# Gated mix of linear attention and expert lookup: where masks, numerators and output matmuls stand from tile 2 on

## The chip, the cores and the metric

The kernel runs on one core of a Trainium2 chip. The metric is the device time of one execution in microseconds (us), the median of several; the profiler adds one execution in which every instruction has a start and an end. The engines are named as in the profile: PE (TensorE matmuls), PEld (its weight loads), DVE (VectorE), ACT (ScalarE), POOL (GpSimd) and SP (SyncE, which here only starts DMAs). PE granted clock 1.00 means the upper of its two levels, 2.4 GHz.

## The reference, cut to what matters

```python
x = A_x                                             # 2048 x 512
g = sigmoid((x * gate_w).sum(-1, keepdims=True))
# A: 32 heads of 16
q, k, v = heads(x @ wqkv)
phi(p) = concat(softmax(p @ w_phi), softmax(-(p @ w_phi)))
kv, z = phi(k)^T @ v, sum_s phi(k)
a = (phi(q) @ kv) / (phi(q) @ z + 1e-6) @ wo
# B: 32 heads, 16 x 16 experts, the best one of each head
i1, i2 = argmax(q1 @ k1^T), argmax(q2 @ k2^T)       # per head
b = sum over heads of gelu(x . u[i1*16+i2]) * v[i1*16+i2]
out = g * a + (1 - g) * b
```

## The kernel before, in words

The 2048 rows are 16 tiles of 128 rows. The first part (to about 150 us of the span) folds weights, accumulates kv and z over all tiles, and builds the score weights. The second part is the loop at L972, one pass for each tile a. Its work is software-pipelined over three tiles: with n = a+1, b = a-1, z = a-2, a pass holds

- `front_q(a)`: the query projection pq, 12 matmuls of 512 columns;
- `front_s(n, 0)` and `front_s(n, 1)`: expert scores of the next tile, two halves of 12 matmuls of 512 columns; `front_p(n)`: 12 matmuls of 258 columns;
- `soft_in`, `soft_exp`, `soft_w`, `soft_sum`, `soft_y`, `soft_p`, `soft_b` for tile a: the dual softmax and the normalizer, on DVE, ACT and POOL;
- `best(n, half)`: the maximum over 16 scores and the equality mask eq, on DVE; `turn_eq(n)` has a DMA transpose eq into et; `mid_mask(a)` turns et into bit masks mk with 8 matmuls of 16 columns on PE, and `count(a, mk)` is a chain of some 17 small DVE steps on those bits that ends in expert counts cf;
- `mid_num(z)`: the numerators oT, 32 matmuls of 64 rows and 128 columns, and their copy by ACT to xh (L781); `num_lo(z)`: the rest xl of that copy, on DVE (L788);
- `back(z)`: the output po, 18 matmuls of 512 columns, of which 12 read xh and xl and 6 the counts; `store(z)` copies po out and starts the DMA.

Everything is in program order on each engine: the kernel writes its schedule out by hand, and an engine runs its instructions in that order and waits for what an instruction needs. PE therefore stops at the first matmul whose operand is missing, whatever stands behind it. The constant DEFER decides how the output is put off: in pass a, `owed` = min(18, 3(a-DEFER)) matmuls of tile z-1's output come first, and all but `left` = min(18, 3(a-DEFER+1)) of tile z's. With DEFER = 8 nothing is put off before pass 8 and all 18 from pass 14.

PSUM banks come from three rings: four for pq, both score halves and pp (and po, where it isn't in the bank called acc), three for mk and the two oT, and acc.

In a pass of before, PE runs pp of the pass before, oT(z), pq(a), po, then (pass 2 to 7) mk(a) and both score halves, or (from pass 8) the first half, mk(a), po, and the second half.

Of the kernel before, what the change touches and what calls it, by code (L numbers as in the profile page):

```python
# [30 lines left out]
DEFER = 8  # L31
# [4 lines left out]
def mix_kernel(ctx, tc, xT, wqT, wkT, wv, wphi, wo, wq, kk, ug, ev, cst, out):  # L36
# [26 lines left out]
    sa = [per.tile([P, 4, 24], U16, name="sa0")]  # L63
# [35 lines left out]
    sa.append(per.tile([P, 4, 24], U16, name="sa1"))  # L99
    sb = [per.tile([P, 4, 24], U16, name=f"sb{i}") for i in range(2)]  # L100
# [592 lines left out]
    def soft_sum(t, i):  # L693
        e = st8[t]
        dve.tensor_reduce(pair(e["st"][:, 64:128])[:, :, i], hs(e["ph"], i), axis=AX.X, op=ALU.add)  # L695
# [7 lines left out]
    def soft_y(t, i):  # L703
        e = st8[t]
        dve.tensor_reduce(pair(e["st"][:, 224:288])[:, :, 1 - i], hs(e["w"], i), axis=AX.X, op=ALU.add)  # L705

    def soft_b(t, step=step):
# [11 lines left out]
        for i in range(2):  # L719
            dve.scalar_tensor_tensor(y[:, :, i], sm[:, :, 1 - i], e["g"][:, 2:3], n_, op0=ALU.mult, op1=ALU.mult)  # L720
# [79 lines left out]
    def count(t, o):  # L800
        e = st8[t]
        A, B = sa[t % 2], sb[t % 2]
        bor = ALU.bitwise_or
        yield dve.tensor_copy(A[:, :, 8:24], o.rearrange("p (g a) -> p g a", a=F))
# [15 lines left out]
        m1w = m1.rearrange("p a b -> p (a b)").bitcast(U32).rearrange("p (w a) -> p w a", a=F)  # L820
        m2w = m2.bitcast(U32).rearrange("p (w b) -> p w b", b=8)
        yield dve.tensor_tensor(x32.rearrange("p (w a b) -> p w a b", w=2, b=8),
                                m1w.unsqueeze(3).to_broadcast([P, 2, F, 8]),
                                m2w.unsqueeze(2).to_broadcast([P, 2, F, 8]), op=band)
# [5 lines left out]
        yield dve.tensor_tensor(T[:, :NX], X[:, :NX], X[:, NX:], op=ALU.add)  # L830
# [130 lines left out]
    def dealt(a, b, z):  # L961
        def first():
            for _ in gate(a):
                step(b)
            step(b, 4)
            if z >= 0:
                back_cl(z)
# [4 lines left out]
    for a in range(NT - 1):  # L972
        n, b, z = a + 1, a - 1, a - 2
        owed = min(18, 3 * max(0, a - DEFER))
        left = min(18, 3 * max(0, a - DEFER + 1))
        B, Z = b >= 0, z >= 0
        if Z:
            mid_num(z)
        if a == 2:
            gelu_pre(a)  # L980
        if a == 1:
            front_q(a)
            v15 = vproj(NT - 1)
            act.copy(woh[3], rawo[3])
        if B:
            planes(b, 0)
            if Z:
                c_join(z)
            if a == 1:
                v15()  # L990
            planes(b, 1)
        if a > 1:
            front_q(a)
        if owed:
            back(z - 1, owed)
            store(z - 1)
        gelu_in(a)
        if Z:
            num_lo(z)
        if B:  # L1000
            if a == 1:
                for _ in gate(a):
                    pass
                soft_in(a)
                dve.tensor_tensor(wol[3], rawo[3], woh[3], op=ALU.subtract)
                step(b, 3)
            else:
                soft_in(a, dealt(a, b, z))
                drain(b)
        else:  # L1010
            for _ in gate(a):
                pass
        if a != 1:
            gelu_act(a)
        if a > 0:
            soft_exp(a)
        if Z and not left:
            back(z)
            store(z)
        if not left and a > 1:  # L1020
            mid_mask(a)
        if a:
            front_s(n, 0)
        if left or a == 1:
            mid_mask(a)
            if 0 < left < 18:
                back(z, 18 - left)
        if a == 1:
# [3 lines left out]
            w4 = ctx.enter_context(tc_pool("w4", "right"))  # L1032
        front_s(n, 1)
        front_p(n, False)
        soft_w(a)
        if a == 1:
            best(n, 0)
        soft_sum(a, 0)
        soft_sum(a, 1)
        if a == 1:  # L1040
            drain(b)
        if a == 0:
            pool.tensor_tensor(wol[2], rawo[2], woh[2], op=ALU.subtract)
            step(a, 5)
        if a != 1:
            best(n, 0)
        if a == 0:
            best(n, 1)
            turn_eq(n)
        soft_y(a, 0)  # L1050
        soft_y(a, 1)
        soft_p(a)
        if B:
# [4 lines left out]
            if a == 1:  # L1058
                gelu_act(a)
        if a == 0:  # L1060
            soft_b(a, lambda t: None)
        else:
# [3 lines left out]
        if a != 1:  # L1066
# [124 lines left out]
```

## Time and profile before

| | |
|---|---|
| median of 3 runs | 375.44 us (374.25 to 375.48) |
| span of the profiled execution, first to last instruction | 371.9 us |
| PE busy | 365.0 us, 98% |
| DVE busy | 332.6 us, 89% |
| ACT busy | 256.3 us, 69% |
| POOL busy | 203.1 us, 55% |
| granted PE clock over the span | 1.00 |

The profile gives the execution by its span; the time of the runs also holds what lies before the first and behind the last instruction, 3.54 us against the median. Busy PE is an average of matmuls that overlap, so a distance from one start to the next says more than a duration.

### The profile page before, as it was taken

The numbers are of one execution on the slowest core, as the hardware profiler recorded it, in microseconds if no ns is written. First come the engines' busy times: TensorE is split into PE (matmuls) and PEld (weight loads), VectorE is DVE, ScalarE is ACT, GpSimd is POOL, SyncE is SP. The second block draws the span as 40 slices with busy tenths as digits, with TensorE's granted clock in tenths as the row PEclk, the third lists the DMA queues.
The fourth block names the chain that finished last, engine by engine and source line by source line (L and its number), as shares of the span: only waits on it lengthen the run. The fifth ranks groups of instructions, "written<-read, shape, count | busy, mean of one in ns | idle before, by whom it ended". The sixth has DMA issues, their size and how long they took to land.

```text
span 371.9 us, 8839 instructions
## 1 busy us (share of the span) xinstructions
PE 365.0 (98%) x3443; PEld 286.2 (77%) x3443; DVE 332.6 (89%) x786; ACT 256.3 (69%) x459; POOL 203.1 (55%) x205
## 2 busy tenths in 40 slices
PE   8999999999999999999999999999999999999995
PEld 4766767777878878777888888878878888888875
DVE  3679999999787979999989999999999999999993
ACT  4585577876666676677868659667786786777641
POOL 1079989988848846443634436426435445454700
PEclk9999999999999999999999999999999999999999
DMA  7868987557882304145264242351452532532201
GB/s 259 321 241 277 252 278 237 173 179 277 279 179 85 89 6 82 24 105 82 61 86 104 57 95 75 85 100 16 114 76 67 115 77 66 115 69 62 70 31 56
DMA packets 72074, 46.67 MB, mean 125 GB/s; under 512 B 63584, under 2 KB 64480, under 8 KB 69728
## 3 DMA queue, kind: packets, MB, share of 16 engines
q1 hardware_dynamic: 71168, 45.24, 45.5%
q10 hardware_dynamic: 864, 0.87, 0.9%
q8 instruction: 27, 0.44, 0.5%
q14 instruction: 15, 0.12, 0.1%
HBM read 26.43 MB, written 4.19 MB: 82 GB/s over the span
## 4 chain that ended last, share of the span: by engine, by line
PE 83%; DVE 5%; POOL 3%; ACT 3%; issue 3%; DMA 2%; SPq 0%; POOLq 0%; ACTq 0%; DVEq 0%
PE po L889 10%; PE s L56 7%; PE s L57 6%; PE s L58 6%; PE po L896 6%; PE pk L459 5%; PE pu L459 4%; PE ws L292 4%; PE pq L56 4%; PE pq L58 3%; PE pq L57 3%; PE oT L777 2%; PE pe L459 2%; PE kvacc L283 2%; PE pv L459 2%
## 5 line engine op out<-in xcount | busy, mean ns | idle before, releaser
L691 POOL TENSOR_TENSOR w<-d,zb 128x512 f32<-128x512 f32 x32 | 40.9, 1297 | 76.8 <-ACT d L685 76.8
L56 PE MATMUL s<-sh,xh 128*128 128x512 f32 x128 | 50.9, 397 | 0.0
L57 PE MATMUL s<-sl,xh 128*128 128x512 f32 x128 | 49.9, 390 | 0.0
L58 PE MATMUL s<-sh,xl 128*128 128x512 f32 x128 | 49.8, 389 | 0.0
L726 POOL TENSOR_TENSOR d<-d,st 128x512 f32<-128x512 f32 x30 | 31.2, 1062 | 28.1 <-DVE st L720 26.5
L685 ACT ACTIVATE d<-d 128x512 f32<-128x512 f32 x32 | 20.0, 632 | 34.2 <-DVE d L119 26.1
L276 POOL TENSOR_TENSOR d<-d,st 128x1024 f32<-128x1024 f32 x16 | 32.5, 2032 | 8.5 <-ACT d L267 6.6
L768 ACT COPY pt<-tp 128x1024 uint16<-128x1024 uint16 x28 | 36.3, 1369 | 0.0
L758 ACT COPY pl<-d 128x1024 uint16<-128x1024 uint16 x28 | 29.2, 1044 | 5.5 <-POOL d L726 5.4
L58 PEld LDWEIGHTS s<-sh,xl 128*128 128x128 f32 x128 | 24.0, 188 | 5.0
L56 PEld LDWEIGHTS s<-sh,xh 128*128 128x128 f32 x128 | 24.0, 188 | 4.7
L57 PEld LDWEIGHTS s<-sl,xh 128*128 128x128 f32 x128 | 24.1, 188 | 4.6
L56 PE MATMUL pq<-wah,xh 128*128 128x512 f32 x64 | 26.8, 418 | 0.0
L58 PE MATMUL pq<-wah,xl 128*128 128x512 f32 x64 | 25.1, 392 | 0.0
L57 PE MATMUL pq<-wal,xh 128*128 128x512 f32 x64 | 25.0, 390 | 0.0
L156 DVE TENSOR_TENSOR xl<-xr,xh 128x512 fp32r<-128x512 f32 (+2 forms) x17 | 21.7, 1288 | 1.7 <-ACT xh L152 1.6
L735 DVE TENSOR_TENSOR eq<-s,mx 128x512 bf16<-128x512 f32 x32 | 22.1, 691 | 1.1
L695 DVE TENSOR_REDUCE st<-d 128x32 f32<-128x512 f32 x32 | 21.5, 680 | 1.4
L734 DVE TENSOR_REDUCE mx<-s 128x32 f32<-128x512 f32 x32 | 21.8, 680 | 0.0
L705 DVE TENSOR_REDUCE st<-w 128x32 f32<-128x512 f32 x32 | 20.5, 677 | 0.6 <-POOL w L691 0.6
L271 DVE TENSOR_REDUCE st<-d 128x64 f32<-128x1024 f32 x16 | 19.4, 1209 | 1.8 <-ACT d L267 1.6
L267 ACT ACTIVATE d<-d 128x1024 f32<-128x1024 f32 x16 | 17.1, 1066 | 4.1 <-DVE d L121 4.1
(272 smaller groups left out, 1119.3 us busy)
## 6 DMA issues: line engine op xcount, KB each, us to landing
wq<-wq SPq DMA_DIRECT2D x16, 1024.0 KB, 5.8
xr<-xT SPq DMA_DIRECT2D x15, 256.0 KB, 5.1
y<-ot SPq DMA_DIRECT2D x15, 256.0 KB, 2.3
rawk<-wkT SPq DMA_DIRECT2D x1, 1024.0 KB, 6.5
rawq<-wqT SPq DMA_DIRECT2D x1, 1024.0 KB, 6.8
rawu<-ug SPq DMA_DIRECT2D x2, 258.0 KB, 5.2
rawv<-wv ACTq DMA_DIRECT2D x2, 256.0 KB, 4.7
rawv<-wv SPq DMA_DIRECT2D x2, 256.0 KB, 5.9
```

Source lines behind the costliest of these rows:

```text
L56: pe.matmul(o, ah, bh, start=(first and i == 0), stop=False)
L57: pe.matmul(o, ah, bl, start=False, stop=False)
L58: pe.matmul(o, al, bh, start=False, stop=(last and i == n - 1))
L276: pool.tensor_tensor(g64(d), g64(d), b64(st[:, 128:192]), op=ALU.mult)
L459: pe.matmul(o, x_, w_, start=(first and i + j == 0), stop=(i == 1 and j == 2), skip_group_check=True)
L691: pool.tensor_tensor(hs(e["w"], i), hs(e["ph"], i), hs(zb, i), op=ALU.mult)
L726: eng.tensor_tensor(g64(d)[:, gs_], g64(d)[:, gs_], r[:, gs_].unsqueeze(2).to_broadcast([P, 32, F]), op=ALU.mult)
L735: dve.tensor_tensor(e["eq"][:, 512 * half:512 * half + 512].rearrange("p (h f) -> p h f", f=F), p3, mx.unsqueeze(2).to_broadcast([P, H, F] ...
L758: act.copy(pl, e["ph"][:, halves[i]].bitcast(U16).rearrange("p (c j) -> p j c", j=2))
L768: act.copy(p16[:, :, 4 * i:4 * i + 4, :], e["tp"][i].rearrange("p (j g) n -> p j g n", j=2))
L889: pe.matmul(po, a, b, start=(i == 0), stop=False)
L896: pe.matmul(po, a, b, start=False, stop=(i == 5))
```

## The change: what it does

Passes 0 and 1 keep their order. From pass 2 on a function `turned(a)` writes the order. DEFER goes from 8 to 2, so 3 more output matmuls are put off in each pass from 2 on, all 18 from pass 8. oT(z) moves from the pass's start to behind the first score half (passes 3 and 4: behind both), with mk(a) right behind it; the ACT copy to xh moves behind `soft_exp(a)`, and `num_lo(z)` on DVE behind `soft_sum(a)`. Pass 2 keeps oT first. In `soft_b` two operations of 32 elements become one of 64; in `count` two exclusive-ors become one on 32-bit words, and an addition reads every second element. po is in the bank acc from tile 0 on.

```diff
-DEFER = 8
+DEFER = 2
...
-        for i in range(2):
-            dve.scalar_tensor_tensor(y[:, :, i], sm[:, :, 1 - i], e["g"][:, 2:3], n_, op0=ALU.mult, op1=ALU.mult)
+        dve.scalar_tensor_tensor(y, sm, e["g"][:, 2:3], n_.unsqueeze(2).to_broadcast([P, H, 2]),
+                                 op0=ALU.mult, op1=ALU.mult)
...
-        dve.tensor_tensor(m1.rearrange("p (w a) j -> p w a j", a=F), twice(A[:, 0:2, 8:24]), twice(A[:, 0:2, 7:23]),
-                          op=ALU.bitwise_xor)
-        yield dve.tensor_tensor(m2.rearrange("p (w a) -> p w a", a=F), A[:, 2:4, 8:24], A[:, 2:4, 7:23],
-                                op=ALU.bitwise_xor)
+        m = w3.tile([P, 2, F], U32, tag="m1", name=f"m{t}")
+        yield dve.tensor_tensor(m, A[:, :, 8:24], A[:, :, 7:23], op=ALU.bitwise_xor)
...
-        yield dve.tensor_tensor(T[:, :NX], X[:, :NX], X[:, NX:], op=ALU.add)
+        x2 = X.rearrange("p (n w) -> p n w", w=2)
+        yield dve.tensor_tensor(T[:, :NX], x2[:, :, 0], x2[:, :, 1], op=ALU.add)
...
+    def turned(a):
+        n, b, z = a + 1, a - 1, a - 2
+        owed = min(18, 3 * max(0, a - DEFER))
+        left = min(18, 3 * max(0, a - DEFER + 1))
+        if a == 2:
+            mid_num(z)
+            gelu_pre(a)
+        planes(b, 0)
+        c_join(z)
+        planes(b, 1)
+        front_q(a)
+        if owed:
+            back(z - 1, owed)
+            store(z - 1)
+        gelu_in(a)
+        if a == 2:
+            num_lo(z)
+        step(b, 0)
+        soft_in(a, dealt(a, b, z))
+        drain(b)
+        gelu_act(a)
+        soft_exp(a)
+        front_s(n, 0)
+        if a < 5:
+            front_s(n, 1)
+        if a > 2:
+            mid_num(z)
+        mid_mask(a)
+        if a >= 5:
+            front_s(n, 1)
+        soft_w(a)
+        soft_sum(a, 0)
+        soft_sum(a, 1)
+        if a > 2:
+            num_lo(z)
+        front_p(n, False)
+        if left < 18:
+            back(z, 18 - left)
+        best(n, 0)
...
+        soft_b(a)
+        best(n, 1)
+        turn_eq(n)
+        gelu_pre(n)
```

On PE, the first row of each group of matmuls in pass 3 of before, from pp of pass 2 to the scores (oT_1 alternates between two banks, 16 matmuls each):

```order
L58 MATMUL pp_2237<-uh,xl_68 128x258
L777 MATMUL oT_1_2296<-pt_2262,kvb 32x128
L777 MATMUL oT_1_2297<-pt_2262,kvb 32x128
...
L56 MATMUL pq_2329<-wah,xh_65 128x512
...
L889 MATMUL po_2376<-t1h,xh_65 128x512
...
L896 MATMUL po_2376<-eh,ch_2322 128x512
...
L796 MATMUL mk_2398<-wm,et_2286 128x16
...
L56 MATMUL s_4_2407<-sh,xh_65 128x512
```

The same pass of the change, from its query projection to the output of tile 1 (po_2227 is tile 0's, po_2420 tile 1's):

```order
L56 MATMUL pq_2296<-wah,xh_65 128x512
...
L891 MATMUL po_2227<-el,ch_2121 128x512
...
L56 MATMUL s_4_2358<-sh,xh_65 128x512
...
L777 MATMUL oT_1_2371<-pt_2250,kvb 32x128
L777 MATMUL oT_1_2372<-pt_2250,kvb 32x128
...
L796 MATMUL mk_2391<-wm,et_2273 128x16
...
L56 MATMUL pp_2407<-uh,xh_65 128x258
...
L884 MATMUL po_2420<-t1h,xh_65 128x512
```

oT and mk now stand side by side, and between oT of tile 1 and the output that reads its copy there are mk and pp, where before there was pq.

On ACT, the copies of oT_1 to xh in before, with what stands around them in passes 2 and 3 (L758 are the planes of the softmax, L685 its exponentials):

```order
L640 ACTIVATE x_2292<-x_2292 128x256
L781 CAST xh_65<-oT_1_2296 128x256
L781 CAST xh_65<-oT_1_2297 128x256
L758 COPY pl_2_2316<-d_2149 128x1024
L852 COPY ctj_2320<-tpc_2269 128x2x256
L856 CAST ch_2322<-ctj_2320 128x256
L758 COPY pl_2_2325<-d_2149 128x1024
```

And in the change:

```order
L758 COPY pl_2_2292<-d_2145 128x1024
L908 COPY ot_2312<-po_2227 128x512
L657 ACTIVATE gs_2275<-gs_2275 128x1
L658 ACTIVATE x_2279<-x_2279 128x256
L659 ACTIVATE x_2279<-x_2279,gs_2275 128x256
L685 ACTIVATE d_2316<-d_2316 128x32x16 x2
L781 CAST xh_65<-oT_1_2371 128x256
L781 CAST xh_65<-oT_1_2372 128x256
```

The copies were ahead of the pass's planes and are now behind its exponentials, which read what DVE writes at L119 and L121 of the same pass; the copy of the stored output (ot) is ahead of them.

## Rows read from the trace of the kernel before

**Rows 1.** The profile's page, its head and the first part: busy us, share, instructions.

```profile
span 371.9 us, 8839 instructions
PE 365.0 (98%) x3443; PEld 286.2 (77%) x3443; DVE 332.6 (89%) x786; ACT 256.3 (69%) x459; POOL 203.1 (55%) x205
```

**Rows 2.** Windows, passes 2 and 4: us, busy PE PEld DVE ACT POOL, clock, DMA.

```profile
151.87:168.59 16.72, 15.51 (x114) 11.93 (x106) 16.21 (x50) 12.64 (x27) 7.51 (x8) 1.00 0.31 72
...
183.49:198.33 14.84, 14.84 (x114) 12.16 (x106) 13.78 (x40) 10.78 (x21) 6.77 (x7) 1.00 0.47 81
```

**Rows 3.** Timeline of PE, pass 2: start us, us, instruction, [idle before, releaser].

```profile
155.50 0.50 PE L889 MATMUL po<-t1h,xh 128*128 128x512 f32 x1 [0.61 <-ACT xh L781]
...
159.12 0.50 PE L896 MATMUL po<-eh,ch 128*128 128x512 f32 x1 [0.60 <-ACT ch L856]
```

**Rows 4.** Timeline of PE around oT, pq, mk and s of pass 5.

```profile
197.52 0.29 PE L58 MATMUL pp<-uh,xl 128*128 128x258 f32 x1
197.74 0.67 PE L777 MATMUL oT<-pt,kvb 64*32 64x128 f32 x32
198.33 0.50 PE L56 MATMUL pq<-wah,xh 128*128 128x512 f32 x1
...
200.97 0.39 PE L58 MATMUL pq<-wah,xl 128*128 128x512 f32 x1
...
205.28 0.36 PE L796 MATMUL mk<-wm,et 128*128 128x16 bf16 x8
205.49 0.47 PE L56 MATMUL s<-sh,xh 128*128 128x512 f32 x1
...
208.08 0.39 PE L58 MATMUL s<-sh,xl 128*128 128x512 f32 x1
```

**Rows 5.** The chain that ended last, one piece in pass 3.

```profile
171.62 2.72 PE po L889 x12
```

**Rows 6.** Timeline of DVE, passes 2 and 3.

```profile
157.12 0.68 DVE L115 TENSOR_REDUCE st<-pq 128x32 f32<-128x512 f32 x1
...
170.74 0.74 DVE L788 TENSOR_TENSOR xl<-oT,xh 128x256 fp32r<-128x256 f32 x2
171.65 0.69 DVE L115 TENSOR_REDUCE st<-pq 128x32 f32<-128x512 f32 x1 [0.17 <-PE pq L58]
```

**Rows 7.** Timeline of ACT, passes 2, 3 and 14.

```profile
155.07 0.65 ACT L781 CAST xh<-oT 128x256 fp32r<-128x256 f32 x2
...
179.07 0.57 ACT L913 COPY ot<-po 128x512 f32<-128x512 f32 x1
...
337.25 0.63 ACT L685 ACTIVATE d<-d 128x512 f32<-128x512 f32 x1 [0.53 <-DVE d L119]
```

**Rows 8.** Timeline of DVE, first instruction of passes 10 and 14.

```profile
274.44 0.68 DVE L115 TENSOR_REDUCE st<-pq 128x32 f32<-128x512 f32 x1
...
331.58 0.68 DVE L115 TENSOR_REDUCE st<-pq 128x32 f32<-128x512 f32 x1
```

**Rows 9.** Timeline of DVE in pass 5, operations that the change merges or alters.

```profile
202.20 0.17 DVE L814 TENSOR_TENSOR m<-sa 128x32 uint16<-128x32 uint16 x1
...
205.57 0.29 DVE L830 TENSOR_TENSOR T<-X 128x256 uint16<-128x256 uint16 x1
...
207.22 0.42 DVE L836 TENSOR_TENSOR cf<-X 128x256 f32<-128x256 uint8 x1
...
213.21 0.42 DVE L720 SCALAR_TENSOR_TENSOR st<-st,gs 128x32 f32<-128x32 f32 x2
```

**Rows 10.** Timelines of DVE and POOL, pass 1, and the same DVE line in pass 5.

```profile
148.72 0.96 DVE L826 TENSOR_TENSOR X<-X,T 128x512 uint16<-128x512 uint16 x1
...
148.66 0.74 POOL L663 TENSOR_TENSOR px<-x,px 128x256 f32<-128x256 f32 x1
...
203.19 0.43 DVE L826 TENSOR_TENSOR X<-X,T 128x512 uint16<-128x512 uint16 x1
```

**Rows 11.** The tile et, the transposes from issue to landing.

```profile
DMA to landing us min/median/max: 2.7/2.7/4.5
```

More of the change, by code (lines that the diff above doesn't have):

```diff
@@ L62, in mix_kernel @@
     ident = cs[:, 0:128]
-    sa = [per.tile([P, 4, 24], U16, name="sa0")]
+    sa = [per.tile([P, 2, 24, 2], U16, name="sa0")]
     wm = per.tile([P, 2, F], BF16, name="wm")
@@ L98, in mix_kernel @@
     kp = per.tile([P, 2, 2, 32], F32, name="kp")
-    sa.append(per.tile([P, 4, 24], U16, name="sa1"))
-    sb = [per.tile([P, 4, 24], U16, name=f"sb{i}") for i in range(2)]
+    sa.append(per.tile([P, 2, 24, 2], U16, name="sa1"))
+    sb = [per.tile([P, 2, 24, 2], U16, name=f"sb{i}") for i in range(2)]
     per.tile([P, 1], F32, name="rest1")
@@ L975, in mix_kernel @@
         left = min(18, 3 * max(0, a - DEFER + 1))
+        if a == 2:
[33 more added lines that the diff above has]
+        best(n, 0)
+        soft_y(a, 0)
+        soft_y(a, 1)
+        soft_p(a)
+        join(b)
+        gelu_out(b)
+        coef(b)
+        c_planes(b)
+        soft_b(a)
+        best(n, 1)
+        turn_eq(n)
+        gelu_pre(n)
+    for a in range(NT - 1):
+        n, b, z = a + 1, a - 1, a - 2
+        if a > 1:
+            turned(a)
+            continue
         B, Z = b >= 0, z >= 0
[L977 to L980, printed above, removed]
         if a == 1:
@@ L984, in mix_kernel @@
             act.copy(woh[3], rawo[3])
-        if B:
[L986 to L1015, printed above, removed]
+            planes(b, 0)
+            v15()
+            planes(b, 1)
+        gelu_in(a)
+        for _ in gate(a):
+            pass
+        if B:
+            soft_in(a)
+            dve.tensor_tensor(wol[3], rawo[3], woh[3], op=ALU.subtract)
+            step(b, 3)
             soft_exp(a)
[L1017 to L1020, printed above, removed]
+            front_s(n, 0)
             mid_mask(a)
[L1022 to L1028, printed above, removed]
             kvacc(NT - 1)
@@ L1032, in mix_kernel @@
             w4 = ctx.enter_context(tc_pool("w4", "right"))
+        else:
+            gelu_act(a)
+        if not B:
+            pass
         front_s(n, 1)
@@ L1039, in mix_kernel @@
         soft_sum(a, 1)
-        if a == 1:
+        if B:
             drain(b)
[L1042 to L1053, printed above, removed]
+            soft_y(a, 0)
+            soft_y(a, 1)
+            soft_p(a)
             join(b)
@@ L1057, in mix_kernel @@
             c_planes(b)
[L1058 to L1062, printed above, removed]
+            gelu_act(a)
             soft_b(a)
@@ L1065, in mix_kernel @@
             turn_eq(n)
-        if a != 1:
+        else:
+            pool.tensor_tensor(wol[2], rawo[2], woh[2], op=ALU.subtract)
+            step(a, 5)
+            best(n, 0)
+            best(n, 1)
+            turn_eq(n)
+            soft_y(a, 0)
+            soft_y(a, 1)
+            soft_p(a)
+            soft_b(a, lambda t: None)
             gelu_pre(n)
```

25 lines of the change are left out of this document (10 added, 15 removed).

## The prediction

> **What bounds the kernel now.** I read the page first: PE is busy for 365.0 of the 371.9 us of the span [rows 1]. That alone does not say that PE is the bound, so I cut the loop at the first pq matmul of each pass. Pass 4 takes 14.84 us, PE without a gap, DVE busy for 13.78, ACT for 10.78 and POOL for 6.77, at a clock of 1.00 [rows 2]. A matmul of 512 columns costs 2.72/12 = 0.227 us from start to start [rows 5]; 54 of them make 12.24 of the 14.84, and 2.60 are left for pp, oT, mk and the places where PE goes from one kind of matmul to another. So in the steady loop only fewer matmuls, or cheaper places of that kind, shorten a pass.
>
> Those places can be read off [rows 4]. From the last pp to oT it is 0.22 us where a pp matmul itself takes 0.12: 0.10 extra. From oT to pq 0.59. The twelve pq then need 2.64 us for eleven distances where 11 x 0.227 = 2.49: 0.15 for getting going again. From mk to the scores 0.21, and those scores need 2.59 for eleven distances: 0.10 again.
>
> Only pass 2 has waits of PE: 0.61 us for xh and 0.60 for the counts' copy ch [rows 3]. With their restarts the pass takes 16.72, that is 1.88 more than pass 4 [rows 2].
>
> DVE is the near second. From pass 10 to pass 14 its first instruction L115 comes every (331.58 - 274.44)/4 = 14.28 us [rows 8], while PE, with three matmuls fewer in those passes, would allow 14.84 - 0.68 = 14.16. So when DVE works without idling, a pass costs it 14.28.
>
> **The change part by part.** I sum against the span of 371.9 us; the median of the runs, 375.44, is 3.54 above it, and I leave these 3.54 as they are.
>
> *DEFER from 8 to 2.* The number of output matmuls stays. 18 of them, 4.08 us, move step by step from passes 2 to 7 into 8 to 13, and the end of the loop owes as many as before, so the last tile's code is unchanged. On PE this is worth nothing by itself. It does two things: pass 2 no longer starts its output behind pq, and a pass from 3 to 7 costs PE 0.68 less, which makes DVE the tighter engine there.
>
> *Pass 2.* pq again starts at 151.87. The scores follow at once; the output of tile 0 comes only behind pp, some 8 us later, when xh and ch are long there. Both waits go: up to 1.88 us. From the row counts: 51 matmuls instead of 54 and no oT(1) in this pass (0.10 + 0.59 + 0.15 = 0.84), so pq of pass 3 starts at 151.87 + 14.84 - 0.68 - 0.84 + 0.15 (pq here still follows oT) = 165.34. mk(2) stands 0.5 us earlier than before and needs et, whose transpose takes 2.7 us [rows 11]; a wait there of up to 0.5 us would be eaten by the next step.
>
> *What is late next: xh in pass 3.* The copy to xh now stands on ACT behind the exponentials, and these wait for DVE. DVE did not win the 1.88 us: before, its last step of pass 2 was L788 at 170.74 for 0.74, and L115 of pass 3 followed at 171.65, having waited only 0.17 for pq [rows 6]. In the change L788 has gone from there (0.74) and the merged operations give some 0.2, so L115 starts at 171.48 - 0.94, about 170.5. From L115 to the slot on ACT behind the exponentials it is 179.07 - 171.65 = 7.42 us [rows 6, 7], and from the start of the copy to the matmul that reads it 155.50 - 155.07 = 0.43 [rows 3, 7]. The output of tile 1 can start at 178.35. PE would be ready for it at 165.34 + 39 x 0.227 (pq, 3 output matmuls, the scores) + 2.60 - 0.15 = 176.65. So PE waits 1.7 us in pass 3, and pp and all else is already behind it. Its pass then ends with 12 matmuls and a restart of 0.15 at 181.22. Before, pq of pass 4 started at 183.49 [rows 2], with 6 matmuls (1.36) and oT(2) (0.69) done that the change still owes: 181.44. Of the 1.88 us, **0.2** remain. If xh came in time, all of it would: these are the two ends, and I take the first, since each link is a row.
>
> *Passes 4 to 14: oT and mk side by side.* Before, PE got going again twice in a pass, behind oT and behind mk. Now mk fills the place behind oT, and one restart goes: the 0.15 of pq. What no row shows is the way from oT to mk. From below it saves nothing (the way costs 0.15 more than 0.59), from above both restarts, 0.25. I take 0.15, for the rest of the sequence is the same rows in another order. 11 passes x 0.15 = **1.65** (0 to 2.75). Pass 3's is lost in its wait.
>
> One rule speaks against this. The Trainium skill, TensorEngine Tiling (Array Packing), Key Properties, says that a change of tiling mode drains the engine. By it the two changes around the 64 x 32 matmuls stay, and the saving would be nothing.
>
> *Does xh hold up PE in later passes?* In pass 4 PE owes 6 matmuls before the scores, so it comes to the output of tile 2 another 0.68 us later, in pass 5 again; DVE at 14.1 against PE's 14.0 falls back by 0.1 a pass. From pass 8 no output stands behind pp at all. So no.
>
> *The small DVE operations.* Per tile: one exclusive-or of 0.17 goes, two operations that take 0.42 together become one (I take 0.25), and the addition that took 0.29 reads every second element; its nearest row is L836, 256 results at one element each time, 0.42, so 0 to 0.13 more [rows 9]. The net is 0.2 (0.2 to 0.35). It shortens DVE's 14.28 to 14.1 and is hidden behind PE in every pass but 2 and 3, where it is in the sum above. Without that cover it would be worth 12 x 0.2 = 2.4.
>
> *Moved on the other queues.* `num_lo` (two instructions) goes behind `soft_sum`, where its xh is there in time; behind it wait best(n, 0) and soft_b, and who waits for them is a pass away. The store's copy stands on ACT ahead of the exponentials and waits for its output; in pass 14 before it stood there too, and the exponential behind it still waited 0.53 for DVE [rows 7]. Its DMA on SP is between the same transposes as before. All at nothing.
>
> Sum: 0.2 + 1.65 = 1.85. The span becomes 370.05 and the time 375.44 - 1.85 = **373.6**.
>
> **The rivals.**
>
> *A. The restart isn't saved.* The switch from oT to mk costs as much as the one to pq and mk keeps its own. For it: weights of another kind and shape must be loaded right behind oT. Then 0.2 remain: 375.2. That is what the rule on tiling modes would give.
>
> *B. PE doesn't wait in pass 3.* For it: only if DVE reaches pass 3 1.7 us sooner, against the row chain above. Then 1.88 + 12 x 0.15 = 3.7: 371.7.
>
> *C. Slower: DVE and POOL collide.* An operation of DVE that reads two SBUF operands took 0.96 us beside one of POOL's and 0.43 alone [rows 10]. Before, POOL's long products lie beside DVE operations that read PSUM or one operand. With L788 away from the end of the pass, POOL's last products reach 0.7 us further into the next, where the count's steps stand. Two collisions cost 2 x 0.53 = 1.06 a pass: DVE at 15.15. It decides from the point where DVE's pass exceeds PE's 14.7 of passes 8 to 14, that is 0.6 of collisions. At 1.06 DVE loses 5 x 1.15 + 7 x 0.45 = 8.9 us, of which its lead over PE's needs covers about 3: 375.44 - 1.85 + 6 = 379.6. Against it: in passes 8 to 14 DVE would wait for pq again, and one collision of 0.3 fits.
> The Trainium skill, SBUF (State Buffer), names this: the pair of ports that VectorE and GpSimd share is locked for a whole instruction, and only certain forms of VectorE need it. The one row agrees; how often it happens in the new order no run here shows.
>
> **How the numbers follow.** 0.5% of this kernel is 1.88 us, about what a measurement can tell from no change. The forecast, 0.60: within its bounds (0.2 to 2.95 saved) 372.5 to 375.2, about evenly on both sides of 373.56. A 0.14, within 0.5%. B 0.16, faster. C 0.10, slower. So faster 0.30 + 0.16 = 0.46, same 0.30 + 0.14 = 0.44, slower 0.10. The range runs from B to A and a little beyond, 371.5 to 375.8, and leaves out C and little more.
>
> **What would show it.** Right: no wait of PE for xh and ch in pass 2; a wait of about 1.7 us for xh at the output of tile 1 in pass 3, and none later; L115 on DVE about 14.1 us apart in passes 4 to 7 and waiting for pq again from pass 9; a pass of 14.7 from pass 8 on PE, 14.0 before; from oT to mk about 0.59. Wrong: oT to mk at 0.75 or more (A); no wait in pass 3 (B); count steps of 0.7 us and more beside POOL and PE waiting from pass 5 on (C); or a wait of PE for et at mk, which stands ahead of the second half of the scores and would hold them up.

## The result, and the profile after

| | before | after |
|---|---|---|
| median of 22 runs each, alternating on one chip | 374.03 us (373.13 to 375.92) | 374.69 us (374.0 to 376.68) |
| ratio after / before, 95% interval | | 1.0024 [1.0013, 1.0036] |
| span of the profiled execution | 371.9 us [rows 1] | 372.2 us |

The change makes the kernel a little slower, where I had forecast 1.85 us less. My 375.44 for before was the median of three runs, and 22 have 374.03; counted from there the forecast was 372.2. (The ratios below leave out one run of 716 us of the last kernel, at twice the time of all the others.) The page of the changed kernel: its head, busy times, and the shares of the chain that ended last.

```profile
span 372.2 us, 8823 instructions
PE 363.8 (98%) x3443; PEld 285.7 (77%) x3443; DVE 336.3 (90%) x754; ACT 254.8 (68%) x459; POOL 204.2 (55%) x205
...
DVE 52%; PE 32%; POOL 5%; ACT 4%; issue 4%; DMA 2%; ACTq 0%; POOLq 0%
```

In the profile of before PE made up 83% of that chain and DVE 5%. Now DVE makes up half, and it is busy for 336.3 us although 32 of its instructions are gone (332.6 in [rows 1]). PE is busy for 1.2 us less, and the span is none the shorter.

First the places of PE that [rows 4] showed: the timeline of PE in pass 6 of after, from the first score half over oT and mk to the second.

```profile
217.40 0.39 PE L58 MATMUL s<-sh,xl 128*128 128x512 f32 x1
217.72 0.67 PE L777 MATMUL oT<-pt,kvb 64*32 64x128 f32 x32
218.32 0.36 PE L796 MATMUL mk<-wm,et 128*128 128x16 bf16 x8
218.53 0.48 PE L56 MATMUL s<-sh,xh 128*128 128x512 f32 x1
218.85 0.40 PE L57 MATMUL s<-sl,xh 128*128 128x512 f32 x1
```

From s to oT 0.32, of which 0.09 is more than a score matmul; oT to mk 0.60; mk to s 0.21; 0.09 for the scores to get going. Together 0.99, where before had 0.10 + 0.59 + 0.15 + 0.21 + 0.10 = 1.15. So 0.16 is saved at this place, as forecast; what went is the 0.15 behind oT, and the 0.09 behind mk is still there.

The waits of PE after, those with a releaser in passes 2 to 15 (those of [rows 3] are gone):

```profile
178.53 0.50 PE L884 MATMUL po<-t1h,xh 128*128 128x512 f32 x1 [2.06 <-ACT xh L781]
...
342.00 0.45 PE L777 MATMUL oT<-pt,kvb 64*32 64x128 f32 x16 [0.75 <-ACT pt L768]
...
346.40 0.66 PE L749 MATMUL pt<-cs,d 128*128 128x128 f32 x4 [0.36 <-DVE gs L649]
```

The first is the one that I forecast, at 178.35 and with 1.7. The other two stand behind the loop, and I had none there. (A wait of 0.52 for ch at the very end is the same in both kernels.)

DVE, to be read against [rows 8]: its first instruction of passes 7, 8, 10 and 14, and between them the count's step L816, with its like in pass 2; then POOL's product beside it.

```profile
157.63 0.42 DVE L816 TENSOR_TENSOR X<-m 128x256 uint32<-128x256 uint32 x1
...
228.65 0.68 DVE L115 TENSOR_REDUCE st<-pq 128x32 f32<-128x512 f32 x1
...
229.54 0.90 DVE L816 TENSOR_TENSOR X<-m 128x256 uint32<-128x256 uint32 x1
...
243.25 0.68 DVE L115 TENSOR_REDUCE st<-pq 128x32 f32<-128x512 f32 x1
...
272.47 0.68 DVE L115 TENSOR_REDUCE st<-pq 128x32 f32<-128x512 f32 x1
...
330.92 0.68 DVE L115 TENSOR_REDUCE st<-pq 128x32 f32<-128x512 f32 x1
```

```profile
229.42 0.74 POOL L653 TENSOR_TENSOR x<-x,px 128x256 f32<-128x256 f32 x1
```

L115 comes every (330.92 - 272.47)/4 = 14.61 us, where I had said 14.1; before it was 14.28. L816 takes 0.90 in each pass from 3 to 14 and 0.42 in passes 1 and 2 and behind the loop: 0.48 more, beside the gelu's product of POOL.

PE's own lead can be read off at its query projections: first pq of pass 14 in before, then pq of passes 2, 4, 8 and 14 in after.

```profile
327.95 0.50 PE L56 MATMUL pq<-wah,xh 128*128 128x512 f32 x1
```

```profile
151.55 0.50 PE L56 MATMUL pq<-wah,xh 128*128 128x512 f32 x1
...
181.40 0.39 PE L56 MATMUL pq<-wah,xh 128*128 128x512 f32 x1
...
237.55 0.39 PE L56 MATMUL pq<-wah,xh 128*128 128x512 f32 x1
...
325.95 0.39 PE L56 MATMUL pq<-wah,xh 128*128 128x512 f32 x1
```

Passes 4 to 7 take (237.55 - 181.40)/4 = 14.04 us and passes 8 to 13 (325.95 - 237.55)/6 = 14.73. The latter have 54 matmuls of 512 columns, as pass 4 of before with its 14.84, so a whole pass gained 0.11 and not 0.16.

At pass 14 pq is 2.00 us earlier; oT(12), which after still owes there, is worth 0.10 + 0.59, which leaves 1.31. Of these, 0.32 lie ahead of the changed passes: pq of pass 2 starts at 151.55, and in before at 151.87 [rows 2]. Such a difference comes with the execution (the profiles of the other kernels have that pq at 151.30 to 153.43, with PE's order up to there the same). So the changed passes had gained PE 0.99. From there to the end after needs 372.2 - 325.95 - 0.69 = 45.56 and before 371.9 - 327.95 = 43.95, so 1.61 are given back behind the loop, 0.62 more than the gain; the medians differ by 0.66. And DVE had hardly gained: from pq of pass 2 to L115 of pass 14 it is 330.92 - 151.55 = 179.37 and before 331.58 - 151.87 = 179.71 [rows 8], but num_lo of that pass (0.74), which before has done by then, is still to come.

### The profile page after: what moved, and what is told of

It is laid out like the page before. It is cut to its first block, busy times and chain, and to the rows that moved or that the text cites. A ratio compares the mean times of both kernels' runs of the same rounds, so it can differ in the third digit from the quotient of the medians.

```text
span 372.2 us, 8823 instructions
## 1 busy us (share of the span) xinstructions
PE 363.8 (98%) x3443; PEld 285.7 (77%) x3443; DVE 336.3 (90%) x754; ACT 254.8 (68%) x459; POOL 204.2 (55%) x205
## 4 chain that ended last, share of the span: by engine, by line
DVE 52%; PE 32%; POOL 5%; ACT 4%; issue 4%; DMA 2%; ACTq 0%; POOLq 0%
DVE eq L735 5%; PE pk L459 5%; DVE mx L734 5%; DVE st L705 5%; PE ws L292 4%; PE pu L459 4%; DVE X L816 3%; DVE xl L788 3%; DVE d L121 2%; PE po L884 2%; DVE st L117 2%; DVE st L115 2%; ACT d L685 2%; DVE st L695 2%; DVE d L119 2%
## 5 line engine op out<-in xcount | busy, mean ns | idle before, releaser
L691 POOL TENSOR_TENSOR w<-d,zb 128x512 f32<-128x512 f32 x32 | 40.9, 1296 | 71.3 <-ACT d L685 71.3
L726 POOL TENSOR_TENSOR d<-d,st 128x512 f32<-128x512 f32 x30 | 31.2, 1060 | 34.1 <-DVE st L719 32.7
L758 ACT COPY pl<-d 128x1024 uint16<-128x1024 uint16 x28 | 29.2, 1044 | 19.1 <-POOL d L726 19.1
L685 ACT ACTIVATE d<-d 128x512 f32<-128x512 f32 x32 | 20.0, 631 | 29.6 <-DVE d L119 21.5
L56 PE MATMUL pq<-wah,xh 128*128 128x512 f32 x64 | 25.3, 395 | 0.0
L705 DVE TENSOR_REDUCE st<-w 128x32 f32<-128x512 f32 x32 | 20.5, 677 | 0.6 <-POOL w L691 0.6
```

The lines of the kernel that those rows point to most:

```text
L56: pe.matmul(o, ah, bh, start=(first and i == 0), stop=False)
L691: pool.tensor_tensor(hs(e["w"], i), hs(e["ph"], i), hs(zb, i), op=ALU.mult)
L705: dve.tensor_reduce(pair(e["st"][:, 224:288])[:, :, i], hs(e["w"], i), axis=AX.X, op=ALU.add)
L726: eng.tensor_tensor(g64(d)[:, gs_], g64(d)[:, gs_], r[:, gs_].unsqueeze(2).to_broadcast([P, 32, F]), op=ALU.mult)
L758: act.copy(pl, e["ph"][:, halves[i]].bitcast(U16).rearrange("p (c j) -> p j c", j=2))
```

## The experiments

Two theories to begin with. **Theory 1**: the collision of L816 with POOL makes DVE the bound of passes 3 to 14, and what PE saves it stands idle for. **The rivals**: the late copies to xh, or the put-off output, cost the time by themselves.

### The collision alone

**The count one place later**, so that L816 isn't beside L653.

```diff
             for _ in gate(a):
-                step(b)
-            step(b, 4)
+                pass
+
+        def second():
+            step(b, 5)
             if z >= 0:
                 back_cl(z, dve)
-        moves = iter((first, lambda: step(b, 5), lambda: step(b, 2), lambda: None))
+        moves = iter((first, second, lambda: step(b, 5), lambda: step(b, 2)))
```

> The change with one edit: on DVE the steps of the count stand one place later in a pass (behind L117, L119 and L121 instead of L115, L117 and L119), so that L117, which reads one operand, lies beside POOL's product L653. Theory 1 (DVE bounds passes 3 to 14, at 14.61 us, because L816 with its two operands in SBUF waits 0.48 beside L653): L816 takes 0.42 again, L115 comes every 14.1 to 14.2 us until it waits for pq, the wait of PE for xh in pass 3 shrinks from 2.06 to about 1.0, the waits of PE at oT and pt behind the loop (0.75 and 0.36) go; 0.993 of before (0.990 to 0.996). Theory 2 (the merged operations themselves are dear here): L816 stays at 0.90 and the time at 1.002. Theory 3 (the loss is the order on ACT behind the loop, not DVE): L115 every 14.1, but the waits behind the loop stay and the time is 1.000 or more.

Measured: 1.0187 [1.0164, 1.0211]. L816 is back to 0.42, but the count's last steps now meet POOL's longer product L691. Timelines of DVE and POOL in pass 7 of this kernel:

```profile
237.15 1.22 DVE L826 TENSOR_SCALAR X<-T 128x128 uint32<-128x128 uint32 x1
```

```profile
237.00 1.28 POOL L691 TENSOR_TENSOR w<-d,zb 128x512 f32<-128x512 f32 x1 [3.56 <-ACT d L685]
```

L826 takes 0.23 elsewhere. Its loss of 1.0 a pass makes L115 15.03 apart, and PE waits 2.66 for xh and 2.20 + 0.69 for pt. The expected time was wrong, since I hadn't looked what stands beside the new place; the mechanism shows all the clearer.

**Half of POOL's product.** The kernel leaves out the other half, so the gelu's argument is unfinished in 128 of 256 columns.

```diff
-        pool.tensor_tensor(x2, x2, px, op=ALU.mult)
+        pool.tensor_tensor(x2[:, :128], x2[:, :128], px[:, :128], op=ALU.mult)
```

> The change with POOL's product L653 cut to 128 of its 256 columns, so the argument of the gelu is left unfinished in half of the columns. Theory 1: L653 takes about 0.4 instead of 0.74 and ends 0.34 sooner, L816 takes 0.55 to 0.6 instead of 0.90, L115 every 14.28 us. Theory 2: L816 stays at 0.90 and L115 at 14.61.

One run: 371.95, below each of the 17 runs of before that stand beside it (373.09 to 375.69, median 373.81). Two first instructions of DVE and the step between them:

```profile
227.57 0.68 DVE L115 TENSOR_REDUCE st<-pq 128x32 f32<-128x512 f32 x1
...
228.46 0.62 DVE L816 TENSOR_TENSOR X<-m 128x256 uint32<-128x256 uint32 x1
...
241.89 0.68 DVE L115 TENSOR_REDUCE st<-pq 128x32 f32<-128x512 f32 x1
```

L653 takes 0.46 for 0.74 and L816 loses only 0.20 for 0.48, so both fall by 0.28; L115 is 14.32 apart, the waits behind the loop are gone, that in pass 3 is 1.42. From pq of pass 2 to the end it is 370.17 - 151.98 = 218.19, where before has 371.9 - 151.87 = 220.03: 1.84 less, the size of my forecast. Nothing but DVE had been held up by this product: ACT reads it at L658, which in pass 7 of the change starts at 232.07, 1.9 behind its end. So DVE's pass sets PE's waits, and with most of the collision gone the gain is there. This is one run of a kernel without all the work.

### The parts of the change alone

**The order (with DEFER 2) with the old small operations**: the pieces of the diff in `soft_b` and `count` undone (two of them here):

```diff
-        dve.scalar_tensor_tensor(y, sm, e["g"][:, 2:3], n_.unsqueeze(2).to_broadcast([P, H, 2]),
-                                 op0=ALU.mult, op1=ALU.mult)
+        for i in range(2):
+            dve.scalar_tensor_tensor(y[:, :, i], sm[:, :, 1 - i], e["g"][:, 2:3], n_, op0=ALU.mult, op1=ALU.mult)
...
-        m = w3.tile([P, 2, F], U32, tag="m1", name=f"m{t}")
-        yield dve.tensor_tensor(m, A[:, :, 8:24], A[:, :, 7:23], op=ALU.bitwise_xor)
+        m1 = w3.tile([P, 32, 2], U16, tag="m1", name=f"m1{t}")
+        m2 = w3.tile([P, 32], U16, tag="m2", name=f"m2{t}")
```

> The order of the change with the small operations of before (two exclusive-ors, two normalizer products, contiguous addition). Theory 1: the wait beside POOL stays (on an exclusive-or or on the bitwise and), about 0.5, so L115 comes every 14.7 to 14.8 us, which is more than PE's 14.73; 1.004 to 1.010 of before. Theory 2: L115 every 14.28 and 0.994 to 0.998 of before.

1.0097 [1.0076, 1.0117]; L115 14.81 apart, PE waits 2.39 for xh and 1.73 + 0.75 for pt. The collision is here too: in passes 3 to 14 the second exclusive-or (L814) takes 0.73 beside L653, and 0.17 in [rows 9].

**The merged operations in the order of before:**

```diff
-DEFER = 2
+DEFER = 8
...
-    def turned(a):
...
+    for a in range(NT - 1):
```

> The order of before with the merged operations of the change. Theory 1: no operation of the count lies beside L653, L816 takes 0.42, L115 every 14.1 to 14.2 where DVE was the tighter engine and PE as before; 0.998 to 1.001 of before. Theory 2: L115 every 14.5 or more from pass 9 on and 1.002 or more.

0.9993 [0.9981, 1.0005]; L816 takes 0.42 in every pass.

**DEFER 2 alone in before:**

```diff
-DEFER = 8
+DEFER = 2
```

> The kernel before with DEFER at 2 and nothing else. Theory 1: the output of tile 0 starts behind the first score half, so the two waits of pass 2 (1.2 us) go at least in part; DVE needs 14.28 a pass from pass 3 on against PE's 14.16, so it falls behind by 0.1 a pass until pass 8 and catches up later; 0.995 to 0.999 of before. If DVE's chain from pass 2 on is the bound whatever PE does: 0.999 to 1.001.

1.0006 [0.9992, 1.002]. The two waits of pass 2 go, and one of 1.76 for et comes at mk in that pass.

So the order costs 1% by itself, and the merged operations are worth 0.0073 of the time (2.7 us) in it, but 0.0007 in the order of before. DVE's pass is 14.81 - 14.61 = 0.20 longer without them, and 12 x 0.2 = 2.4 was what I gave for "without that cover"; what is left of the 2.7 can be PE's clock, which was low in all runs of the order alone and in half of those of the change (last section).

### The collision cured by num_lo, and the copies to xh

**num_lo back at the pass's end** in passes 5 to 13:

```diff
-        if a > 2:
+        if 2 < a < 5 or a == NT - 2:
             num_lo(z)
...
         turn_eq(n)
+        if 5 <= a < NT - 2:
+            num_lo(z)
         gelu_pre(n)
```

> The change with one edit: in passes 5 to 13 the numerators' rest (L788, two operations on DVE that read PSUM) goes back to the end of the pass, ahead of the next L115, where it stood before; passes 3, 4 and 14 keep it behind the softmax sums. Theory 1 (an operation of the count that reads two SBUF operands waits for POOL's product L653; DVE's pass then bounds passes 3 to 14): L653 is over before L816 starts, L816 takes 0.42 in passes 6 to 14, L115 comes every 14.15 to 14.25 us until it waits for pq, no wait of PE behind the loop; 0.993 to 0.997 of before. If the collision were not what lengthens DVE's pass (the copy's place, the merged operations): L115 stays at 14.5 or more and the time at 1.000 to 1.003.

1.0011 [0.9998, 1.0024]. L816 is 0.42 from pass 6, L115 14.17 apart until it waits for pq again, and nothing is left behind the loop. But PE waits 1.99 for xh in pass 3 and, in pass 6, 1.01 for xl: the output put off from pass 5 reads xl there, and num_lo now is the last step of that pass on DVE.

**The copies to xh ahead of the exponentials** in passes 3 and 4, alone and with num_lo late:

```diff
-        soft_exp(a)
         front_s(n, 0)
         if a < 5:
             front_s(n, 1)
-        if a > 2:
+        if 2 < a < 5:
+            mid_num(z)
+        soft_exp(a)
+        if a >= 5:
             mid_num(z)
```

> The change with one edit: in passes 3 and 4 the copy to xh stands on ACT ahead of the exponentials, so that the output of tile 1 need not wait for DVE. Theory 1 (DVE's chain bounds the time from pass 3 to the end of the loop): PE's wait of 2.06 us in pass 3 goes, L115 still comes every 14.61, PE waits for as much somewhere later (et, or behind the loop), and the time is that of the change, 1.000 to 1.004 of before. Rival (PE's wait in pass 3 is what ate the gain): 0.995 to 0.998 of before.

> Both edits: the numerators' rest late in passes 5 to 13 and the copy to xh early in passes 3 and 4. Theory 1: with L115 every 14.2 DVE catches up with PE's 14.72 in passes 8 to 14, so that the wait taken away in pass 3 is kept this time; 0.989 to 0.994 of before, up to 2 us below the kernel with the late rest alone. If DVE doesn't catch up before the loop ends: the same time as with the late rest alone.

Alone 1.0011 [0.9997, 1.0025]: the wait moves to xl (0.96 in pass 3) and xh (0.49 in pass 5), and 0.76 + 0.36 stay behind the loop. Both: 0.9996 [0.9982, 1.001]: waits of 0.99, 0.50 and 1.26, none behind the loop. Curing one place brings the kernel back to the time of before, and the gain that I expected of it did not come.

### Another share of the put-off output

In passes 2 to 8 three matmuls are put off, then 6 to 18 up to pass 13, so that PE's passes stay as long as DVE's; then the same with xh early in passes 3 and 5 to 9.

```diff
-        owed = min(18, 3 * max(0, a - DEFER))
-        left = min(18, 3 * max(0, a - DEFER + 1))
+        off = lambda p: min(18, 3 * max(1, p - 7)) if p > 1 else 0
+        owed, left = off(a - 1), off(a)
```

> The change with another table for what is put off: 3 matmuls in passes 2 to 8, then 6, 9, 12, 15, and 18 from pass 13, so that from pass 3 PE has 54 matmuls of 512 columns (14.69 us) as long as DVE is behind, not 51. Theory 1 with its second half (PE gains nothing in passes that DVE bounds, and matmuls put off there come back in passes that PE bounds): PE waits about 2 us for xh in pass 3 as before, the lag of DVE behind pq is then under 1 us through the whole loop, the waits behind the loop (0.75 and 0.36) go although L816 still takes 0.90 and L115 comes every 14.61 or slower with pq; 0.994 to 0.998 of before. If only the collision beside POOL costs the gain: the time of the change, 1.001 to 1.004.

> The same table, and the copy to xh ahead of the exponentials in passes 3 and 5 to 9. Theory 1: the wait in pass 3 falls from 2.06 to about 1.0 (xl is then what is late), none follows, and this time nothing takes the us back; 0.991 to 0.996 of before, 0.002 to 0.003 below the even table alone. Rival (DVE's chain from pass 2 to the end of the loop is the bound even then): the same as the even table alone.

1.0066 [1.0045, 1.0087] and 1.0030 [1.0019, 1.0041]. In the first, DVE and PE go at the same 14.83 up to pass 9, and the collision is still there: a step of DVE's timeline in pass 6, and one in pass 11.

```profile
215.63 0.70 DVE L811 TENSOR_TENSOR m<-sa 128x32 uint32<-128x32 uint32 x1
...
289.60 0.89 DVE L816 TENSOR_TENSOR X<-m 128x256 uint32<-128x256 uint32 x1
```

In passes 4 to 9 DVE idles 0.06 to 0.10 for pq ahead of L115, and the exclusive-or L811 (0.19 elsewhere) meets L653; from pass 10 it is L816 again. Either way 0.5 are lost in each pass, since POOL's products, L653 the last of them, follow DVE's L719. PE's short passes now come last, and no time is left for DVE to make them good: 0.40 + 0.75 and 0.36 of waits behind the loop. In the second PE waits 1.00 for xl in pass 3 and 0.64 for xh in pass 4, and 0.27 + 0.74 and 0.36 behind the loop.

**The change with DEFER at 8**, so that nothing is put off before pass 8. This kernel leaves out the store of tiles 0 to 5, and their po is in the ring of four banks again.

```diff
-DEFER = 2
+DEFER = 8
```

I had expected 0.997 to 1.003. Measured: 1.0098 [1.0075, 1.0121].

```profile
163.91 0.47 PE L884 MATMUL po<-t1h,xh 128*128 128x512 f32 x1 [1.99 <-DVE d L121]
```

L121 reads pq and not po, so this wait in pass 2 is taken to be one for its bank. Passes 3 to 7 take PE 14.98, and DVE waits 0.6 to 0.8 for pq in each; there L816 takes 0.42, and from pass 10, where DVE no longer waits, it takes 0.90 again. So the put-off output isn't what costs the change its gain, as far as this kernel shows: without it the new order is 2.1 us slower than the change from pq of pass 2 to the end (374.5 - 151.74 = 222.76 against 220.65), and DEFER 2 alone had cost nothing.

### All the work, POOL's product moved

**L653 right behind L663 on POOL**, with the gelu's copies ahead of the join on ACT and a third buffer for its operands:

```diff
-        px = w2.tile([P, NX], F32, name=f"px{t}", tag="px")
-        x2 = w2.tile([P, NX], F32, name=f"x2{t}", tag="x2")
+        px = w2.tile([P, NX], F32, name=f"px{t}", tag="px", bufs=3)
+        x2 = w2.tile([P, NX], F32, name=f"x2{t}", tag="x2", bufs=3)
...
+        gelu_pre(n)
         join(b)
         gelu_out(b)
+        if n < NT - 1:
+            gelu_in(n)
         coef(b)
```

> The change, whole in its work, but with the gelu's operands copied from pp by ACT ahead of the join of pt (they get a third buffer each, since the expert coefficients still read the old one) and POOL's product L653 issued right behind L663, ahead of the counts' product, so that it lies beside DVE's sums L705 and no longer behind soft_b's products and beside L816. Theory 1 (the collision of L816 with L653 is what DVE pays, and DVE's pass is what PE pays): L816 back to 0.42, L115 about 14.13 apart from pass 4 on, no wait of PE behind the loop, 1.4 to 1.7 us for xh in pass 3, and 0.993 to 0.997 of the time before. Rival 2 (a DVE operation with two SBUF operands always meets some POOL product in this order, so it only moves): an operation of 0.7 us and more elsewhere in the pass, L115 at 14.5 or more, 1.001 to 1.006. Rival 3 (without any collision PE still waits for what DVE and ACT hand it in passes 3 to 8, as in the two runs with num_lo late): L115 at 14.2 and waits of 2.5 us and more in all, 0.999 to 1.001.

> The kernel with POOL's gelu product ahead, and the copies of oT to xh of passes 3 and 4 ahead of ACT's exponentials. If the wait for xh in pass 3 is the only loss that is left (theory 1): it falls to 0.9 to 1.5 us, counting what appears for xl behind it, and the ratio is 0.001 to 0.002 below the other run's. If that wait is only the lateness of DVE and moves to xl whole (rival 3): the ratio of the other run within 0.001.

1.0126 [1.0108, 1.0144] and 1.0108 [1.0082, 1.0134]. L816 is cured and L700 hurt: 0.20 became up to 0.75, here in pass 6 beside the counts' product, and L115 is 14.73 apart from pass 5 on.

```profile
225.07 0.75 DVE L700 SCALAR_TENSOR_TENSOR st<-st 128x32 f32<-128x32 f32 x1
```

```profile
225.01 0.74 POOL L835 TENSOR_TENSOR cf<-cf,px 128x256 f32<-128x256 f32 x1
```

Most of the loss is at another place: the join is late in pass 14, PE waits 2.71 + 0.72 for it, and its clock falls (last section).

**L653 behind the counts' product**, the last pass as in the change; then with xh early in passes 3 and 4:

```diff
-        gelu_pre(n)
+        if n < NT - 1:
+            gelu_pre(n)
         join(b)
         gelu_out(b)
+        coef(b)
         if n < NT - 1:
             gelu_in(n)
-        coef(b)
```

> As the run with POOL's gelu product ahead, but L653 behind the counts' product L835 on POOL, so that both lie beside DVE's sums L705 and the first operation with two SBUF operands behind them, L700, comes when they are done; and the last pass keeps the change's order, so that the join of pt isn't late for oT(13). Theory 1 (DVE's pass without collisions is some 14.15, and the predicted gain is there then): L700 0.20 and L816 0.42 in most passes, L115 about 14.15 apart, one wait of 1.4 to 1.8 for xh in pass 3, nothing or less than 0.5 behind the loop, clock 1.00, 0.993 to 0.997 of the time before. Rival (L700 still meets a product now and then): L115 at 14.3 to 14.6, waits behind the loop, 0.999 to 1.005.

> The same with the copies of oT to xh of passes 3 and 4 ahead of ACT's exponentials. Theory 1: the wait in pass 3 falls to about 0.8 (for xl), 0.001 to 0.003 below the other run's ratio, that is 0.991 to 0.996. Rival: as the other run or worse, since pass 4 starts later for DVE.

1.0045 [1.0023, 1.0066] and 0.9995 [0.9979, 1.0011]. Now hardly a collision is left (L816 0.42 throughout, L700 0.19 in all passes but one and two): free of them DVE's passes 3 and 4 take 14.13 and 14.14 in the first of the two, the 14.1 of the prediction, and from pass 8 DVE goes at PE's 14.7. Of the second kernel: PE's pq of pass 14, its waits behind the loop, and a new one of DVE, that comes in each of the late passes.

```profile
325.76 0.39 PE L56 MATMUL pq<-wah,xh 128*128 128x512 f32 x1
...
340.94 0.45 PE L777 MATMUL oT<-pt,kvb 64*32 64x128 f32 x16 [0.30 <-ACT pt L768]
342.16 0.45 PE L777 MATMUL oT<-pt,kvb 64*32 64x128 f32 x16 [0.76 <-ACT pt L768]
```

```profile
289.72 0.43 DVE L872 TENSOR_TENSOR cl<-ctj,ch 128x256 fp32r<-128x256 f32 x1 [0.44 <-ACT ch L851]
```

Its pq of pass 2 is at 152.27, 0.40 later than in before, so in the changed passes PE gained 327.95 - 325.76 - 0.69 + 0.40 = 1.90, and the kernel still ends at 372.4. PE's gain is real, and behind the loop it is lost: with some 0.5 of idle time for ch in each late pass DVE is as slow as with the collision.

### The end behind the loop

The last pq ahead of oT(13), and 12 output matmuls ahead of the transposes of pt(14), in the change and in the last kernel:

```diff
-    mid_num(z)
     c_join(z)
     front_q(a)
+    mid_num(z)
+    back(z - 1, 12)
     mid_phi(b)
...
-    back(z - 1)
+    back(z - 1, 6)
     store(z - 1)
```

> The change, with another order behind the loop: the last query projection ahead of oT(13) on PE, as in the loop's passes, and 12 of the output matmuls of tile 12 ahead of the transposes of pt(14). Theory 1 (the wait of oT(13) for pt and the 0.36 behind it are where the saving of the loop is lost, since DVE's late pass 14 sets the end of the join): both waits gone with their restarts, 1.2 to 1.8 us: 0.998 to 1.000 of the time before, with L115 still 14.6 apart. Rival (what is late behind the loop only moves to the next matmul that needs it, by DVE's own chain to the end): 1.001 to 1.003, and a wait of 1 us and more at pt(14), oT(14) or oT(15).

> The same end with POOL's gelu product behind the counts' product and the xh copies of passes 3 and 4 early, so without the collisions. Theory 1: the loop's 1.5 us are kept and the end loses nothing: 0.993 to 0.997 of the time before. Rival as in the other run: 0.998 to 1.001.

1.0036 [1.0021, 1.0052] and 1.0011 [0.9995, 1.0028]: the rival, though the wait is at none of the three places that I named. The waits for pt go, and the same time is spent further on. The end of the counts of tile 14 on DVE and the matmul that reads them, in the second of these kernels and in before:

```profile
359.62 0.42 DVE L835 TENSOR_TENSOR cf<-cf,px 128x256 f32<-128x256 f32 x1
...
360.10 0.71 PE L863 MATMUL CT<-cs,cf 128*128 128x128 f32 x4 [1.74 <-DVE cf L835]
```

```profile
358.87 0.43 DVE L840 TENSOR_TENSOR cf<-cf,px 128x256 f32<-128x256 f32 x1
...
360.36 0.71 PE L868 MATMUL CT<-cs,cf 128*128 128x128 f32 x4
```

A matmul CT starts 0.06 behind cf when it waits. So in before 360.36 - 359.36 = 1.0 us lay between PE and a wait for DVE there. It is not the tightest place. The transposes of pt(14) on PE, where the change waits 0.36, read the last of POOL's products L726, and these follow DVE's L719 (L720 in before). That product and the second four transposes in before, then the product in the change:

```profile
344.96 1.06 POOL L726 TENSOR_TENSOR d<-d,st 128x512 f32<-128x512 f32 x1
```

```profile
346.09 0.64 PE L749 MATMUL pt<-cs,d 128*128 128x128 f32 x4
```

```profile
345.28 1.06 POOL L726 TENSOR_TENSOR d<-d,st 128x512 f32<-128x512 f32 x1
```

In the change the product ends at 346.34 (as does L649, which the profile names) and the transposes start at 346.40, 0.06 behind it. In before it ends at 346.02 and they start at 346.09: PE comes there 0.01 us later than it could. So whatever PE alone gains ahead of this place is idle time, unless DVE's pass 14 ends sooner, or other matmuls are put ahead of it as in these two kernels; then the next bound is CT. And DVE did not end sooner: from pq of pass 2 to cf it is 207.43 in before (cf at 359.30), 207.93 in the change (359.48), 207.37 with L653 behind the counts and xh early (359.64), 208.19 here. With half of the product it is 205.44, 2.0 less, and that is the kernel that was faster:

```profile
356.99 0.43 DVE L835 TENSOR_TENSOR cf<-cf,px 128x256 f32<-128x256 f32 x1
```

## Why the prediction was wrong, step by step

- **Pass 2: right.** Both waits are gone. Its length from pq to pq is 165.01 - 151.55 = 13.46; 165.34 - 151.87 = 13.47 was the sum.
- **xh late in pass 3: right in place and cause, 0.36 too small.** 2.06 for 1.7. From pq of pass 2 to that of pass 4 it is 181.40 - 151.55 = 29.85, where 181.44 - 151.87 = 29.57 was the forecast's measure of before: all of the 1.88 is eaten and 0.3 more.
- **oT and mk side by side: right at the place, too large over the pass.** 0.16 for 0.15, and oT to mk 0.60; but a whole pass gained 0.11 (14.84 to 14.73), so 11 of them 1.2 and not 1.65. The rule of the Trainium skill, TensorEngine Tiling (Array Packing), Key Properties, that a change of tiling mode drains the engine, agrees with the 0.60, which the switch to pq had cost too; that nothing could be saved, as I read it, the trace refutes: the restart of 0.15 behind oT went.
- **The small operations: the step that failed.** "It shortens DVE's 14.28 to 14.1 and is hidden behind PE in every pass but 2 and 3." The merged prices are in order: the exclusive-or takes 0.19 and the product of 64 elements 0.29, and the strided addition 0.42 for 0.29. But 14.61 was the pass, since one collision of 0.48 came back every time. Three runs show that it is this: with half the product 14.32, with the product elsewhere 14.13 (passes 3 and 4), with the collision at a longer product 15.03. And the DVE pass was no side matter: where it fell to 14.32, the forecast gain came (1.84 us, one run).
- **Rival C: its mechanism, dismissed by a wrong bound.** I wrote that it "decides from the point where DVE's pass exceeds PE's 14.7" and that "one collision of 0.3 fits". A pass of 14.61 stays below 14.7 and decided all the same, since PE's passes 4 to 7 are 14.04 long here. DVE falls behind by 0.57 in each of them, 2.3 in four, and wins back 0.1 in each pass from 8 on. Putting off output matmuls shortened PE's pass just where DVE could not follow.
- **"No waits later": wrong.** I looked at xh alone. What DVE's lag makes late behind the loop is the join of pt, which stands on ACT behind the exponentials (0.75), and POOL's product for the transposes of pt(14), behind L719 (0.36); with what PE loses around these waits it is 1.6.
- **A bound that I had left out.** A term that shortens PE counts only as far as the end allows. At pt(14) before had 0.01 us between PE and a wait for POOL and DVE, and 1.0 at CT, so the sum of PE's terms was worth nothing without a DVE that ends sooner. It fits that no kernel with all the work came out below before by more than its interval. Merging alone, which brings cf to 358.86, is one of these: 0.9993.

What stays open: whether a kernel with all the work that has PE's saving, no collision, and an earlier end of DVE is faster. None of those here has all three; the one with half of the product comes nearest, with a single run. Each cure of the collision brought a wait of its own (for xl, for ch, for the join), so how much of the miss the collision makes and how much the end is not shown apart.

## What to carry to other kernels

Where two engines are within a few per cent of each other, a saving on the one is worth no more than the slack of the other at the end of the chain: measure that slack (when an operand is ready, and when it is read, at each place behind the loop) ahead of summing savings per pass. When an order is changed, list what POOL runs beside each two-operand DVE step in its new place, and price one meeting times the passes: in the change it came in all 12 passes, and in before in none of these. Undo the parts one at a time: here the merged operations were worth 2.7 us inside the new order and 0.3 outside it.

## What the runs showed of the hardware

**A DVE step that meets POOL's product can have to wait it out, whatever its own size.** L816 (0.42) became 0.90 and ended 0.28 behind the end of a POOL product of 0.74; L826 (0.23) became 1.22 and ended 0.09 behind one of 1.28; L700 (0.20) became 0.75 and ended 0.07 behind one of 0.74. What is lost is what is left of POOL's product when DVE arrives, less some 0.14: 0.62 left and 0.48 lost, 1.13 and 0.99, 0.68 and 0.55, and with half of the product 0.34 and 0.20. Not every step waits: the sum L705, with one operand, takes its 0.67 beside a product too (239.28 in the change, beside L835). The Trainium skill, SBUF — State Buffer (Who interferes with whom), has it that the pair of ports that VectorE and GpSimd share is locked for a whole instruction, against VectorE operations with two SBUF inputs or in a two-port mode; the rows of L816 and L700 (two inputs) agree, and L826 reads one operand, so it would be of the second kind, which no row here shows.

**After a wait of about 2 us PE often comes back at its lower clock.** The windows of the kernel with L653 ahead, behind PE's waits of 2.71 and 0.72, and two of its matmuls there (us; busy PE, PEld, DVE, ACT, POOL; clock):

```profile
345.00:348.00 3.00, 3.00 (x15) 2.29 (x8) 1.49 (x5) 1.33 (x3) 2.87 (x4) 0.50 0.86 91
```

```profile
345.73 0.63 PE L57 MATMUL pq<-wal,xh 128*128 128x512 f32 x1
346.15 0.63 PE L58 MATMUL pq<-wah,xl 128*128 128x512 f32 x1
```

Half the clock is 1.2 GHz of 2.4; the matmuls are 0.42 apart and not 0.23. It doesn't always come: the change and the change with another end have the same wait in pass 3 (2.06 and 2.04), and behind it the clocks of these two profiled executions differ; first the change, then the other.

```profile
180.00:184.00 4.00, 4.00 (x19) 3.30 (x18) 3.96 (x15) 3.01 (x8) 1.49 (x3) 1.00 0.15 35
```

```profile
180.00:184.00 4.00, 4.00 (x12) 3.13 (x12) 3.97 (x15) 3.38 (x8) 1.47 (x3) 0.60 0.15 35
```

In these 4 us PE has 12 matmuls where there had been 19. Each run's granted clock over the span shows how often this was so:

| kernel | longest wait of PE in the loop or behind it (profiled execution), us | runs below a clock of 0.997 |
|---|---|---|
| before | 0.61 | 0 of 125 |
| merges alone; xh early; both cures by num_lo; put-off even, xh early; L653 behind the counts, xh early | 0.62; 0.96; 1.26; 1.00; 0.82 | 0 of 12 each |
| half of the product | 1.42 | 0 of 1 |
| DEFER 2 alone | 1.76 | 3 of 12 |
| L653 behind the counts | 1.89 | 8 of 11 |
| num_lo late; the change with DEFER at 8 | 1.99; 1.99 | 6 of 12; 3 of 4 |
| put-off even | 2.03 | 2 of 6 |
| the change; with another end | 2.06; 2.04 | 11 of 22; 9 of 12 |
| L653 behind the counts, xh early, another end | 1.74, at CT | 7 of 11 |
| the order alone; the count later; L653 ahead; L653 ahead, xh early | 2.39; 2.66; 2.71; 2.71 | all of 6, 5, 5, 6 |

The change's 11 runs at a clock of 0.997 and more have a median of 374.46, the other 11 one of 375.3. So 0.8 us of what it loses in half its runs goes with the lower clock, a price that the prediction didn't have; the runs without it are no faster than before either.
